# Score matmuls of half the height for the first 8 pairs and of full height for the rest, x^T of two batches by DMA, and a table of urgencies, in a kernel of attention and a gated MLP

## The chip, the cores and the metric

One core of a Trainium2 chip. The metric is the device time of one execution in microseconds (us); a comparison uses the median of several runs. Of the engines, TensorE (PE) does the matmuls, VectorE (DVE), ScalarE (ACT) and GpSimd (POOL) the work on their results, and SyncE (SP) issues transfers. PE's clock is granted at one of two levels, 1.2 or 2.4 GHz; the profile gives it as a share of 2.4 GHz.

## The reference

q, k and v have the shape [4, 8, 768, 64]: 4 batches of 8 heads. Each query keeps the 6 chunks of 32 keys with the greatest upper bound on the score, computed from each chunk's smallest and greatest key. The result feeds a gated MLP.

```python
k_min = np.min(k_chunks, axis=3); k_max = np.max(k_chunks, axis=3)
ub = np.sum(np.maximum(q[:, :, :, None, :] * k_min[:, :, None, :, :],
                       q[:, :, :, None, :] * k_max[:, :, None, :, :]), axis=-1)
ub = np.where(causal, ub, -1e9)
top_chunks = np.argsort(ub, axis=-1)[..., -6:]
scores = scale * np.matmul(q, k.transpose(0, 1, 3, 2))     # kept where selected and causal
x = softmax(scores) @ v                                    # then [4, 768, 512]
h = gelu(x @ w_in)                                         # w_in [512, 1024]
u, v = h[..., :512], h[..., 512:]
v_n = (v - mean(v)) / sqrt(var(v) + 1e-6) * g_ln
v_s = einsum('ts,bsd->btd', w_sg, v_n) + b_sg              # w_sg [768, 768]
out = x + (u * v_s) @ w_out                                # w_out [512, 512]
```

## The kernel before

The work is written as operations (`P.op`), each with an engine, an estimated cost, the data that it reads and writes, and a priority. `Program.schedule` plays them through with these costs: whenever an engine is free, it starts the operation that can start first, and among those within 0.02 us of it the one with the smallest priority. That gives one fixed order for each engine; `link` adds the semaphore waits that the data need. So the order on the chip is decided ahead, and where the costs are off, an engine waits in that order. Each engine takes its instructions in order, the transfers that SP or POOL issue included.

The heads are taken in pairs (16 pairs, one head in partitions 0 to 63, the other in 64 to 127) and in quads of two pairs. The steps of a pair:

- `loads`: k, q and v of two heads, six transfers of SP. There are 3 buffers of each kind, and at most 4 loads are in flight.
- `kside`, `qside`: PE transposes in f32; DVE takes minimum and maximum of the chunks (W), ACT copies to KT (bf16) and qT (f32), DVE makes rT, POOL casts qT to QT. `vside`: POOL casts v to vx.
- `select`, for a quad: bounds on PE with tiles of 64 x 32, then on DVE transposition, the 6th greatest value of each query (`max`), a comparison and a transposition to Dt: 24 rows for each head, 1 where a chunk is not selected.
- `scores`: for six pieces (`PIECES`) of the causal triangle, K^T Q over 64 rows, and on top of it a matmul of the indicator IND (-BIG for the keys of a chunk) with Dt, also over 64 rows. The two heads of a pair use the two halves of PE's rows. Queries below LO = 192 need no mask. ACT takes the exp of each piece into E; POOL zeroes what lies over the diagonal.
- `head`: 21 matmuls of E with v, then DVE divides into XS. `xtrans`: x^T of a pair, 6 PE transposes and a DVE copy to xT.

After the four pairs of a batch come `moe_h` (hv and hu with w_in, gelu on ACT, statistics and vhat on DVE, one step on POOL for rstd) and `moe_g` (the matmul with w_sg, two DVE steps to uT, the matmul with w_out, the sum with XS, the output). The buffers of MoE are double, by the batch's parity. The priorities are 100 for each quad, plus fixed offsets:

```python
                if g % 2 == 0:
                    b = g // 2 - 1
                    P.base = 100.0 * (g - 1) + 150.0 + 40
                    moe_h(b)
                    P.base = 100.0 * (g - 1) + 150.0 + 150
                    moe_g(b)
```

`weights(h)` issues the transfers of w_in, w_sg and w_out on POOL's queue, two for a head, once the first exp of the pair is done ("tick"); the bias and g_ln go by SP. Until the first scores PE runs matmuls on zeros in its free time (`fill`).

Of the kernel before, what the change touches and what calls it, by code (L numbers as in the profile page):

```python
# [43 lines left out]
class Op:  # L44
    __slots__ = ("eng", "fn", "cost", "prio", "deps", "dma", "ps", "alloc", "table", "burst",
                 "start", "end", "pos", "waits", "inc", "count", "idx", "lane", "bulk", "port")


class Program:
# [54 lines left out]
    def schedule(self):  # L104
# [23 lines left out]
        table = None  # L128
        burst_left = {}
# [18 lines left out]
        soft_free = 0.0  # L148
        flight = []
        held = {"pool": 0.0, "dve": 0.0}  # L150
        while n < len(ops):
            pick = None
            for e in ENGINES:
# [22 lines left out]
                best = min((c for c in cands if c[0] <= tmin + 0.02), key=lambda c: c[1])  # L176
# [16 lines left out]
            cost = o.cost  # L193
            if e == "act" and o.table is not None:
# [180 lines left out]
def pe(cols, n=1):  # L375
    return max(cols / 2400.0, n * 0.027)


def _kernel(nc, q, k, v, w_in, g_ln, w_sg, b_sg, w_out, out):
# [24 lines left out]
    for c_, ps_ in enumerate(PIECES):  # L404
# [5 lines left out]
        ELEN.append(o_)  # L410

    with contextlib.ExitStack() as ctx:
# [12 lines left out]
        XS = T("XS", [128, 2 * NT, DM], BF16)  # L425
# [7 lines left out]
        DIRECT = 4  # L433
        qn = [T(f"qn{i}", [128, NT, 2, DH], F32) for i in range(NQS)]
# [3 lines left out]
        rT = [T(f"rT{i}", [128, NSEL], F32) for i in range(4)]  # L438
# [3 lines left out]
        KT = [T(f"KT{i}", [128, S], BF16) for i in range(4)]  # L442
        QT = [T(f"QT{i}", [128, S], BF16) for i in range(4)]
# [3 lines left out]
        Dt = [T(f"Dt{i}", [128, NSEL], BF16) for i in range(2)]  # L447
        E = [[T(f"E{i}_{c}", [128, 2, n], BF16) for c, n in enumerate(ELEN)] for i in range(2)]
# [47 lines left out]
        def weights(h):  # L496
            after = [("tick", h)]
            for i in (2 * h, 2 * h + 1):
                if i < 4:
                    P.op("pool", lambda g, i=i: g.dma_start(  # L500
                        winb[:, i, :], bass.AP(w_in.tensor, 128 * DFF * i, [[DFF, 128], [1, DFF]])), 2.0,
                        reads=after, writes=[("winb", i)], dma=f"winb{i}")
                elif i < 10:
                    j = i - 4
                    P.op("pool", lambda g, j=j: g.dma_start(
                        wsgf[j], bass.AP(w_sg.tensor, 128 * S * j, [[S, 128], [1, S]])), 1.6,
                        reads=after, writes=[("wsgf", j)], dma=f"wsgf{j}")
# [376 lines left out]
```

## Time and profile before

| | |
|---|---|
| median of 3 runs | 266.33 us (264.33 to 268.38) |
| the profiled execution | 266.45 us |
| its span, first to last instruction | 264.7 us |
| busy: PE / DVE / ACT / POOL | 232.8 / 188.9 / 148.7 / 70.8 us |
| moved by DMA | 28.72 MB, 109 GB/s over the span |

Busy time is the time in which an engine has work in it; matmuls overlap, so a busy PE may still have room. A chain of waits followed back from the last instruction tells which work ended last at each step.

### The profile page before, as it was taken

The page shows a single profiled execution, that of the slowest core. Times are in us where ns is not written, and L with a number is a line of the kernel's source. Part 1 is how long each engine was busy: PE and PEld are TensorE (multiplying, and loading weights), DVE is VectorE, ACT ScalarE, POOL GpSimd, SP SyncE. Part 2 cuts the span into 40 slices and gives each one's busy share as a digit, 9 for nine tenths or more (in the row PEclk, how much of TensorE's full clock was granted, in tenths as well). Part 3 has the DMA queues.
Part 4 walks back from the last instruction along what each step waited for, and adds up shares of the span by engine and source line. Part 5 has one row for each costly group of instructions (what it writes and reads, how often), then busy time and mean ns, then how long its engine had stood idle before and what let it go on. Part 6 is the DMA issues. An engine that isn't in the chain of part 4 may idle for free.

```text
span 264.7 us, 6262 instructions
## 1 busy us (share of the span) xinstructions
PE 232.8 (88%) x2534; PEld 132.1 (50%) x2551; DVE 188.9 (71%) x541; ACT 148.7 (56%) x224; POOL 70.8 (27%) x95
## 2 busy tenths in 40 slices
PE   8998788698999999988977999978988998689884
PEld 3554455546546665455534765544435565434431
DVE  3659666478769978867597768866687776447783
ACT  1316799268549658477655857197674554736000
POOL 4135551936120423225021313143011021001000
PEclk9999999599999999999999999999999999979999
DMA  7999999998983166865022050210000032100033
GB/s 165 208 226 207 219 221 200 194 235 185 220 177 88 34 198 147 215 156 122 5 59 59 2 178 2 82 41 4 2 0 0 5 119 81 40 0 0 2 119 120
DMA packets 81437, 28.72 MB, mean 109 GB/s; under 512 B 76416, under 2 KB 77696, under 8 KB 81408
## 3 DMA queue, kind: packets, MB, share of 16 engines
q1 hardware_dynamic: 79392, 25.57, 40.6%
q0 software_dynamic: 2016, 2.75, 6.2%
q8 instruction: 20, 0.33, 0.5%
q14 instruction: 9, 0.07, 0.1%
HBM read 24.77 MB, written 6.29 MB: 117 GB/s over the span
## 4 chain that ended last, share of the span: by engine, by line
PE 51%; DMA 16%; DVE 14%; issue 8%; ACT 7%; SPq 1%; POOL 1%; POOLq 1%; DVEq 0%
DMA kn<-in_k_dram 11%; PE PSG L767 8%; PE PSG L787 8%; PE PSG L674 6%; PE PSC L633 6%; DMA vn<-in_v_dram 5%; PE PSG L723 5%; PE PSG L595 5%; DVE vhat L739 5%; PE PSC L639 4%; PE PSG L542 3%; DVE vsT L774 3%; DVE uT L778 2%; ACT E_1 L649 2%; PE PSG L695 2%
## 5 line engine op out<-in xcount | busy, mean ns | idle before, releaser
L633 PE MATMUL PSC<-QT,KT 64*128 64x128 bf16 (+3 forms) x384 | 40.3, 265 | 8.3 <-ACT E_1 L649 2.4
L548 DVE TENSOR_REDUCE W<-PSG 128x12 f32<-128x384 f32 x64 | 32.7, 541 | 8.3 <-PE PSG L542 8.2
L767 PE MATMUL PSG<-wsgT,vhat 128*128 128x384 bf16 x192 | 35.3, 327 | 3.4 <-DVE vhat L739 3.3
L639 PE MATMUL PSC<-Dt,IND 64*128 64x128 bf16 (+5 forms) x352 | 37.8, 260 | 0.0
L633 PEld LDWEIGHTS PSC<-QT,KT 64*128 64x128 bf16 x384 | 17.1, 95 | 28.5 <-issue 7.3
L657 POOL TENSOR_SCALAR_AFFINE_SELECT E_0<-E_0 128x1024 bf16<-128x1024 bf16 x16 | 17.9, 1121 | 39.0 <-ACT E_0 L649 39.0
L576 POOL CAST QT<-qT 128x768 bf16<-128x768 f32 x16 | 14.2, 895 | 49.2 <-PE PSC L639 25.3
L649 ACT ACTIVATE E_1<-PSC 128x1024 bf16<-128x1024 f32 x16 | 16.4, 1024 | 17.7 <-PE PSC L639 17.7
L649 ACT ACTIVATE E_0<-PSC 128x1024 bf16<-128x1024 f32 x16 | 16.6, 1035 | 17.1 <-PE PSC L639 17.1
L774 DVE SCALAR_TENSOR_TENSOR vsT<-PSG,glnT,bsgbc 128x384 f32<-128x384 f32 x32 | 19.6, 612 | 9.0 <-PE PSG L767 8.9
L767 PEld LDWEIGHTS PSG<-wsgT,vhat 128*128 128x128 bf16 x192 | 17.2, 98 | 17.6 <-ACT uT L754 2.7
L787 PE MATMUL PSG<-woutb,uT 128*128 128x512 bf16 x88 | 22.2, 380 | 3.7 <-DVE uT L778 3.0
L749 PE MATMUL PSG<-xT,winb 128*128 128x384 bf16 x128 | 24.1, 327 | 0.1
L723 PE MATMUL PSG<-winb,xT 128*128 128x512 bf16 x89 | 22.2, 391 | 1.6 <-DVE xT L699 1.1
L793 DVE TENSOR_TENSOR osb<-PSG,XS 128x512 f32<-128x512 f32 x24 | 16.4, 689 | 8.9 <-PE PSG L787 8.7
L727 ACT ACTIVATE vgb<-PSG 128x512 f32<-128x512 f32 x24 | 14.0, 596 | 15.4 <-PE PSG L723 15.4
L551 ACT ACTIVATE KT<-PSG 128x384 bf16<-128x384 f32 x32 | 15.3, 497 | 11.7 <-DVE W L548 11.6
L649 ACT ACTIVATE E_3<-PSC 128x1024 bf16<-128x1024 f32 x16 | 16.5, 1031 | 6.9 <-PE PSC L639 6.9
L570 ACT ACTIVATE qT<-PSG 128x384 f32<-128x384 f32 x32 | 15.1, 504 | 9.3 <-PE PSG L565 9.3
L580 POOL CAST vx<-vn 128x768 bf16<-128x768 f32 x16 | 13.6, 848 | 24.6 <-PE PSG L674 14.1
L754 ACT ACTIVATE uT<-PSG 128x384 bf16<-128x384 f32 x32 | 15.7, 490 | 7.9 <-PE PSG L749 7.4
L649 ACT ACTIVATE E_4<-PSC 128x1024 bf16<-128x1024 f32 x16 | 16.6, 1037 | 6.2 <-PE PSC L639 6.1
(77 smaller groups left out, 449.1 us busy)
## 6 DMA issues: line engine op xcount, KB each, us to landing
kn<-in_k_dram SPq DMA_DIRECT2D x32, 192.0 KB, 3.6
qn<-in_q_dram SPq DMA_DIRECT2D x32, 192.0 KB, 3.7
vn<-in_v_dram SPq DMA_DIRECT2D x32, 192.0 KB, 3.6
out_dram<-osb SPq DMA_DIRECT2D x24, 256.0 KB, 2.0
winb<-in_moe_w_in_dram POOLq DMA_DIRECT2D x4, 256.0 KB, 5.5
vhat<-in_moe_w_sg_dram POOLq DMA_DIRECT2D x3, 192.0 KB, 4.6
uT<-in_moe_w_sg_dram POOLq DMA_DIRECT2D x3, 192.0 KB, 5.7
woutb<-in_moe_w_out_dram POOLq DMA_DIRECT2D x4, 128.0 KB, 6.3
```

Of the source, the lines that this page charges most:

```text
L548: P.op("dve", lambda d, t=t, m=m, op=op, hf=hf: d.tensor_reduce(W[w][:, m, 12 * hf:12 * hf + 12], t.ap()[:, 0:TG].rearrange("p (c x) -> p ...
L633: r = e.matmul(t.ap()[:, 512 * i + o:512 * i + o + n], KT[w][rows, 128 * kb:128 * kb + 128], QT[w][rows, q0:q0 + n], start=first, stop=(q0 ...
L639: r = e.matmul(t.ap()[:, 512 * i + o + m0 - q0:512 * i + o + n], ind[rows, 128 * kb:128 * kb + 128], Dt[u][rows, m0 - LO:q0 + n - LO], sta ...
L649: P.op("act", lambda e, t=t, c=c, n=n: e.activation(E[es][c][:], t.ap()[:, 0:1024].rearrange("p (i x) -> p i x", x=512)[:, :, 0:n], ACTF.E ...
L657: P.op("pool", lambda g, ev=ev, m=m: g.affine_select(ev, ev, pattern=[[0, 2], [0, m], [1, 128]], compare_op=ALU.is_ge, fill=0.0, base=0, c ...
L674: r = e.matmul(t.ap()[:, 65 * qb:65 * qb + 65], E[es][c][:, i, o:o + 128], vx[w][:, kb, i, :], start=first, stop=(c == 0), skip_group_chec ...
L723: r = e.matmul(t.ap()[:, 0:F], xT[s][:, dk, 128 * qt:128 * qt + 128], winb[:, dk, F:DFF], start=(dk == 0), stop=(dk == NDK - 1))
L749: r = e.matmul(t.ap()[:, 0:TG], winb[:, dk, 128 * fb:128 * fb + 128], xT[s][:, dk, TG * tg:TG * tg + TG], start=(dk == 0), stop=(dk == NDK ...
L767: r = e.matmul(t.ap()[:, 0:TG], vhat[s][:, sb, 128 * fb:128 * fb + 128], wsgT[:, sb, TG * tg:TG * tg + TG], start=(sb == 0), stop=(sb == N ...
L774: P.op("dve", lambda d, t=t, fb=fb, tg=tg, vs=vs: d.scalar_tensor_tensor(vsT[vs][:], t.ap()[:, 0:TG], glnT[:, fb:fb + 1], bsgbc[:, TG * tg ...
L787: r = e.matmul(t.ap()[:, 0:DM], gT[s][:, fb, 128 * qt:128 * qt + 128], woutb[:, fb, :], start=(fb == 0), stop=(fb == NF - 1))
L793: P.op("dve", lambda d, t=t, qt=qt, os_=os_: d.tensor_tensor(osb[os_][:], t.ap()[:, 0:DM], XS[:, (b % 2) * NT + qt, :], op=ALU.add), dve(D ...
```

## The change

- `scores` stays for the pairs 0 to 7 (SIDE = 8). From pair 8 on `scores_one` works on one head at a time: the first head's operands KA and QA hold K^T or Q^T in rows 0 to 63 and the indicator or Dt in rows 64 to 87, the second head's KB and QB hold them in rows 64 to 127 and in rows 0 to 23 (the rest is zero), so one matmul gives score and mask. The rows that come from other partitions are copied by SP: KB, the indicator, QB, and two of Dt, five transfers for a pair. A head has three tiles (1024, 1024 and 640 columns), the diagonal blocks first, and E is one buffer.
- x^T of the batches 2 and 3 is made by `dma_start_transpose` on SP, but for the last slice of batch 3. XS has the blocks of 128 features outside.
- A table URGENCY gives each step of each pair or batch its own priority, in place of the fixed offsets.
- The weights: each pair releases a list (WHEN), and the bias and g_ln are released by pair 2.
- The plan's constants: latencies, costs of operations and transfers, a cost for a change between kinds of matmul (MODE_SWITCH), and a tolerance for each engine (SLACK) within which the priority decides. rT has two buffers in place of four.

```diff
-LAT = {"pe": 0.15, "act": 0.20, "dve": 0.12, "pool": 0.15, "sp": 0.05}
+LAT = {"pe": 0.15, "act": 0.25, "dve": 0.12, "pool": 0.15, "sp": 0.05}
+SLACK = {"pe": 0.15, "act": 0.1, "dve": 0.1, "pool": 0.3, "sp": 0.02}
 TABLE_SWITCH = 1.3
+MODE_SWITCH = 0.095
...
-                best = min((c for c in cands if c[0] <= tmin + 0.02), key=lambda c: c[1])
+                best = min((c for c in cands if c[0] <= tmin + SLACK[e]), key=lambda c: c[1])
...
+            if e == "pe" and o.mode != mode:
+                cost += MODE_SWITCH
+                mode = o.mode
...
-                if e == "pool":
-                    soft_free = max(soft_free, t + 1.0) + 2.0 * cost
-                    dma_free = max(dma_free, t + 0.3) + 0.4 * cost
-                else:
-                    dma_free = max(dma_free, t + 0.3) + cost
-                free[e] = max(t + 0.6, dma_free - 3.0) if e == "sp" else t + 0.9
-                o.end = (soft_free if e == "pool" else dma_free) + 2.0
+                dma_free = max(dma_free, t + (1.0 if e == "pool" else 0.2)) + cost
+                free[e] = t + (0.9 if e == "pool" else 0.5)
+                o.end = dma_free + (2.2 if e == "pool" else 1.6)
...
+WHEN = [(0, 1), (2, 3, 4, 5), (6, 7, 8, 9, 14), (10, 11, 12, 13)]
+URGENCY = {
+        "load": [21, 1, 120, 126, 221, 388, 525, 392, 525, 361, 529, 668, 611, 889, 862, 904],
+        "k": [320, 143, 76, 123, 147, 316, 75, 314, 315, 432, 551, 578, 604, 684, 879, 859],
+        "q": [30, 132, 97, -60, 230, 303, 441, 411, 1100, 493, 579, 1201, 1307, 1169, 1501, 1463],
+        "loadv": [-95, 74, 163, 188, 369, 485, 389, 414, 630, 365, 923, 913, 1121, 705, 597, 897],
+        "v": [-64, -18, 111, -54, 217, -39, 255, 47, 223, 239, 571, 414, 620, 954, 1074, 1042],
+        "sel": [59, 94, 184, 412, 259, 490, 252, 594],
+        "sc": [133, 165, 273, 364, 398, 448, 500, 430, 429, 771, 686, 924, 1027, 1076, 919, 955],
+        "pv": [189, 319, 361, 325, 520, 489, 535, 637, 840, 1086, 1098, 1136, 1309, 1349, 1344, 1305],
+        "xt": [-417, -44, -42, 194, -297, 173, 130, -226, 110, 773, 703, 802, 893, 1227, 1006, 1369],
+        "wsg": [-130],
+        "hv": [43, 609, 856, 831],
+        "hu": [404, -196, 1218, 1970],
+        "pt": [617, 508, 743, 1334, 1292, 1441, 2245, 1650],
+        "out": [423, 540, 506, 541, 584, 822, 1099, 421],
+}
...
+    ECUT = [(0, 1024), (1024, 2048), (2048, 2688)]
+    ETOT = 2688
+    FOFF = []
+    acc = S
+    for kb_ in range(NT - 1):
+        FOFF.append(acc)
+        acc += S - 128 * (kb_ + 1)
...
+        for u in range(2):
+            P.op("dve", lambda d, u=u: d.memset(Dt[u][:, 0:LO], 0.0), 0.1, writes=[("Dt0", u)])
+        for i in range(4 if SIDE < 16 else 0):
+            P.op("pool", lambda g, i=i: g.memset(QB[i][0:64, :], 0.0), 0.5, prio=400.0, writes=[QB[i].name + "D"])
+            P.op("pool", lambda g, i=i: g.tensor_copy(KB[i][0:64, :], IND[0][0:64, :]), 0.8, prio=400.0,
+                 reads=["IND0"], writes=[KB[i].name + "I"])
...
-        def weights(h):
-            after = [("tick", h)]
-            for i in (2 * h, 2 * h + 1):
+        def weights(p):
+            after = [("tick", p)]
+            for i in WHEN[p]:
...
-            if h == 1:
-                P.op("sp", lambda s: s.dma_start(bsgbc[:], bass.AP(b_sg.tensor, 0, [[0, 128], [1, S]])),
-                     1.5, writes=["bsgbc"], dma="bsg")
-                P.op("sp", gln_load, 0.3, writes=["glnT"], dma="gln")
+                else:
+                    P.op("sp", lambda s: s.dma_start(bsgbc[:], bass.AP(b_sg.tensor, 0, [[0, 128], [1, S]])),
+                         2.3, reads=after, writes=["bsgbc"], dma="bsg")
+                    P.op("sp", gln_load, 0.3, reads=after, writes=["glnT"], dma="gln")
...
+            if p < SIDE:
+                return
+            P.op("sp", lambda e: e.dma_start(KB[w][64:128, :], KA[w][64:128, :]), 0.4,
+                 reads=[("KAI", w)], writes=[("KB", w)], dma=f"kb{w}")
+            P.op("sp", lambda e: e.dma_start(KA[w][64:64 + NC, :], IND[0][0:NC, :]), 0.2,
+                 reads=["IND0", ("KB", w)], writes=[("KAI", w)], dma=f"ki{w}")
...
+            if p >= SIDE:
+                P.op("sp", lambda e: e.dma_start(QB[w][64:128, :], QA[w][64:128, :]), 0.4,
+                     reads=[("QAD", w)], writes=[("QB", w)], dma=f"qb{w}")
...
+            for j in range(4):
+                p = 2 * g + j % 2
+                w = p % 4
+                if p < SIDE:
+                    continue
+                qt_, lo, key = (QA[w], 64, ("QAD", w)) if j < 2 else (QB[w], 0, QB[w].name + "D")
+                P.op("sp", lambda e, j=j, qt_=qt_, lo=lo: e.dma_start(qt_[lo:lo + NC, :],
+                                                                      Dt[u][32 * j:32 * j + NC, :]), 0.2,
+                     reads=[("Dt", u), ("Dt0", u)] + ([("QB", w)] if j < 2 else []), writes=[key],
+                     dma=f"D{w}_{j // 2}")
...
+        def scores_one(p, i):
+            w, es = p % 4, p % 2
+            kt_, qt_, rows = (KA[w], QA[w], slice(0, 64 + NC)) if i == 0 else (KB[w], QB[w], slice(0, 128))
+            rd = [("KA", w, 0), ("KA", w, 1), ("KAI", w), ("QA", w), ("QAD", w)] if i == 0 else \
+                [("KB", w), KB[w].name + "I", ("QB", w), QB[w].name + "D"]
+            pieces = [(128 * kb, 128, kb, 128 * kb) for kb in range(NT)]
+            pieces += [(FOFF[kb], S - 128 * (kb + 1), kb, 128 * (kb + 1)) for kb in range(NT - 1)]
+            for c, (c0, c1) in enumerate(ECUT):
+                t = ps_score.tile()
+                mms = []
+                for (e0, n, kb, q0) in pieces:
+                    a, z = max(e0, c0), min(e0 + n, c1)
+                    while a < z:
+                        y = min(z, c0 + ((a - c0) // 512 + 1) * 512)
+                        mms.append((a - c0, y - a, kb, q0 + a - e0))
+                        a = y
+
+                def sc(e, t=t, mms=mms):
+                    for (o, n, kb, q0) in mms:
+                        r = e.matmul(t.ap()[:, o:o + n], kt_[rows, 128 * kb:128 * kb + 128],
+                                     qt_[rows, q0:q0 + n], start=True, stop=True, skip_group_check=True)
+                    return r
+                P.op("pe", sc, sum(max(m_[1], 66) for m_ in mms) / 2400.0 + 0.03, reads=rd, writes=[t], alloc=t)
+                P.op("act", lambda e, t=t, c0=c0, c1=c1: e.activation(
+                    E[es][:, ETOT * i + c0:ETOT * i + c1], t.ap()[:, 0:c1 - c0], ACTF.Exp, scale=SCALE),
+                    act(c1 - c0), reads=[t], writes=[("E", es, 3 * i + c)], ps=[t], table="exp")
+            ev = E[es][:, ETOT * i:ETOT * i + S].rearrange("p (j x) -> p j x", x=128)
+            P.op("pool", lambda g: g.affine_select(ev, ev, pattern=[[0, NT], [1, 128]], compare_op=ALU.is_ge,
+                                                   fill=0.0, base=0, channel_multiplier=-1), gps(S),
+                 reads=[("E", es, 3 * i)], writes=[("E", es, 3 * i)])
 
...
+            r, w = [("XS", b % 2, 2 * dk), ("XS", b % 2, 2 * dk + 1)], [("xT", b % 2, dk)]
+            if b >= XDMA and not (dk == NDK - 1 and b == B - 1):
+                P.op("sp", lambda e: e.dma_start_transpose(
+                    xT[b % 2][:, dk, :].rearrange("p (j x) -> p j x", x=128),
+                    XS[:, b % 2, dk].rearrange("p j x -> p (j x)")), 1.0, reads=r, writes=w, dma=f"x{dk}")
+                return
...
+                for p in (2 * g - 2, 2 * g - 1):
+                    at("sc", p)
+                    if p < SIDE:
+                        scores(p)
+                    for i in range(2):
+                        if p >= SIDE:
+                            at("sc", p)
+                            P.base += 10 * i
+                            scores_one(p, i)
+                        at("pv", p)
+                        P.base += 10 * i
+                        head(2 * p + i)
+                    if p < len(WHEN):
+                        P.base = 0.0
+                        weights(p)
+                    if p == 3:
+                        at("wsg", 0)
                         for sb in range(NT):
                             wsg_trans(sb)
-                    if h % 2 == 1:
-                        P.base += 5
-                        xtrans(h // H, (h % H) // 2)
+                    at("xt", p)
+                    xtrans(p // 4, p % 4)
```

## Rows read from the trace of the kernel before

**Rows 1.** The page: busy time by engine, and PE's granted clock in 40 slices.

```profile
PE 232.8 (88%) x2534; PEld 132.1 (50%) x2551; DVE 188.9 (71%) x541; ACT 148.7 (56%) x224; POOL 70.8 (27%) x95
...
PEclk9999999599999999999999999999999999979999
```

**Rows 2.** Stretch, length; busy PE, PEld, DVE, ACT, POOL; PEclk, DMA share, GB/s.

```profile
22.00:66.00 44.00, 36.52 (x535) 23.24 (x537) 30.63 (x100) 31.50 (x49) 25.15 (x35) 0.92 1.06 210
47.00:57.00 10.00, 8.49 (x112) 5.40 (x114) 5.37 (x12) 3.73 (x5) 8.17 (x13) 0.66 1.11 207
66.00:228.00 162.00, 148.40 (x1709) 85.44 (x1720) 122.64 (x348) 101.41 (x150) 37.72 (x42) 1.00 0.33 84
228.00:264.70 36.70, 27.73 (x178) 12.98 (x178) 22.88 (x46) 9.82 (x17) 1.32 (x1) 0.95 0.11 44
```

**Rows 3.** The chain that ended last: start us, us, what.

```profile
37.71 7.39 DMA vn<-in_v_dram
45.12 3.30 DMA kn<-in_k_dram
...
242.49 2.84 DVE vhat L739 x6
```

**Rows 4.** Waits, 22 to 66 us: who for whom, us, times, longest.

```profile
POOL vx L580 <- DMA vn<-in_v_dram: 7.5, 1, 7.5
...
PE PSG L542 <- DMA kn<-in_k_dram: 3.0, 1, 3.0
```

**Rows 5.** Waits from 228 us to the end.

```profile
PE PSG L787 <- DVE uT L778: 2.4, 2, 1.6
...
PE PSG L723 <- DVE xT L699: 1.1, 1, 1.1
```

**Rows 6.** Timeline of PE, 223 to 226 us: start, length, what, count.

```profile
224.18 0.27 PE L633 MATMUL PSC<-QT,KT 64*128 64x256 bf16 x2
224.29 0.27 PE L639 MATMUL PSC<-Dt,IND 64*128 64x256 bf16 x2
224.50 0.30 PE L674 MATMUL PSG<-vx,E_2 128*128 128x65 bf16 x4
...
225.03 0.29 PE L674 MATMUL PSG<-vx,E_0 128*128 128x65 bf16 x4
225.25 0.39 PE L633 MATMUL PSC<-QT,KT 64*128 64x512 bf16 x2
```

**Rows 7.** Timeline of PE: first and last of 28 runs of scores.

```profile
113.73 0.23 PE L633 MATMUL PSC<-QT,KT 64*128 64x128 bf16 x2
...
226.98 0.34 PE L633 MATMUL PSC<-QT,KT 64*128 64x384 bf16 x2 [0.27 <-ACT E_2 L649]
```

**Rows 8.** Timeline, transposes of batch 2's last slice to hv.

```profile
183.18 0.51 PE L695 MATMUL PSG<-identB,XS 128*128 128x128 bf16 x6
...
183.62 0.69 PE L595 MATMUL PSG<-qT,W 64*32 64x288 f32 x8
...
184.95 0.81 PE L723 MATMUL PSG<-winb,xT 128*128 128x512 bf16 x3 [0.16 <-issue]
```

**Rows 9.** Groups by line: the copy to xT; busy us, mean ns | idle.

```profile
L699 DVE COPY xT<-PSG 128x768 bf16<-128x768 bf16 x16 | 8.9, 555 | 6.2 <-PE PSG L695 5.9
```

**Rows 10.** Outputs (L796): time from issue to landing.

```profile
DMA to landing us min/median/max: 2.0/2.0/3.1
```

**Rows 11.** Loads of q, k and v (L527): time to landing.

```profile
DMA to landing us min/median/max: 2.5/3.6/10.3
```

**Rows 12.** Timeline: Dt of pairs 8 and 9, pair 8's first score.

```profile
115.88 0.78 DVE L618 STREAM_TRANSPOSE Dt<-Dn 128x576 bf16<-128x576 bf16 x1
...
118.21 0.28 PE L633 MATMUL PSC<-QT,KT 64*128 64x128 bf16 x4 [0.63 <-ACT E_4 L649]
```

**Rows 13.** Waits of SP's queue.

```profile
SPq L527 <- POOL vx L580: 13.1, 2, 10.9
```

More of the change, by code (lines that the diff above doesn't have):

```diff
@@ L45 @@
     __slots__ = ("eng", "fn", "cost", "prio", "deps", "dma", "ps", "alloc", "table", "burst",
-                 "start", "end", "pos", "waits", "inc", "count", "idx", "lane", "bulk", "port")
+                 "start", "end", "pos", "waits", "inc", "count", "idx", "lane", "bulk", "port", "mode")
 class Program:
@@ L128, in schedule @@
         table = None
+        mode = "full"
         burst_left = {}
@@ L437, in _kernel @@
         qT = [T(f"qT{i}", [128, S], F32) for i in range(4)]
-        rT = [T(f"rT{i}", [128, NSEL], F32) for i in range(4)]
+        rT = [T(f"rT{i}", [128, NSEL], F32) for i in range(2)]
         W = [T(f"W{i}", [128, 2, 32], F32) for i in range(4)]
@@ L441, in _kernel @@
         vx = [T(f"vx{i}", [128, NT, 2, DH + 1], BF16) for i in range(4)]
-        KT = [T(f"KT{i}", [128, S], BF16) for i in range(4)]
-        QT = [T(f"QT{i}", [128, S], BF16) for i in range(4)]
+        KA = [T(f"KA{i}", [128, S], BF16) for i in range(4)]
+        KB = [T(f"KB{i}", [128, S], BF16) for i in range(4)]
+        QA = [T(f"QA{i}", [128, S], BF16) for i in range(4)]
+        QB = [T(f"QB{i}", [128, S], BF16) for i in range(4)]
         U = [T(f"U{i}", [128, NBLK, 32], F32) for i in range(2)]
@@ L645, in scores @@
                 n = ELEN[c]
[L646 to L647 removed]
+                P.op("pe", sc, 2 * n / 2400.0 + 0.02, mode="rows",
+                     reads=[("KA", w, 0), ("KA", w, 1), ("QA", w), ("Dt", u), "IND0", "IND0b", "IND1"],
                      writes=[t], alloc=t)
[L649 to L650 removed]
+                ev = E[es][:, off:off + 2 * n].rearrange("p (i x) -> p i x", i=2)
@@ L651, in scores @@
+                off += 2 * n
+                P.op("act", lambda e, t=t, n=n, ev=ev: e.activation(
+                    ev, t.ap()[:, 0:1024].rearrange("p (i x) -> p i x", x=512)[:, :, 0:n], ACTF.Exp,
                     scale=SCALE), act(2 * n), reads=[t],
-                    writes=[("E", es, c)] + ([("tick", 2 * p), ("tick", 2 * p + 1)] if c == 0 else []), ps=[t],
-                    table="exp")
+                    writes=[("E", es, c)] + ([("tick", p)] if c == 0 else []), ps=[t], table="exp")
@@ L665, in head, with block @@
             t = ps_g.tile((3,) if h < H else (2, 3))
-            def pv(e):
-                first = True
-                for c in (2, 3, 4, 5, 1, 0):
-                    for kb, q0, n in PIECES[c]:
-                        for x in range(0, n, 128):
-                            qb = (q0 + x) // 128
-                            o = EOFF[kb, qb][1]
-                            r = e.matmul(t.ap()[:, 65 * qb:65 * qb + 65], E[es][c][:, i, o:o + 128],
-                                         vx[w][:, kb, i, :], start=first, stop=(c == 0), skip_group_check=True)
-                            first = False
-                return r
-            P.op("pe", pv, 21 * 0.03, reads=[("E", es, c) for c in range(6)] + [("vx", w), ("vx1", w)],
+            def block(kb, qb):
+                if p >= SIDE:
+                    return ETOT * i + (128 * qb if kb == qb else FOFF[kb] + 128 * (qb - kb - 1))
+                c, o = EOFF[kb, qb]
+                return 2 * sum(ELEN[:c]) + ELEN[c] * i + o
+            order = [(kb, qb) for kb in range(NT) for qb in range(kb + 1, NT)] + [(kb, kb) for kb in range(NT)]
+            def pv(e):
+                for n, (kb, qb) in enumerate(order):
+                    o = block(kb, qb)
+                    r = e.matmul(t.ap()[:, 65 * qb:65 * qb + 65], E[es][:, o:o + 128], vx[w][:, kb, i, :],
+                                 start=(n == 0), stop=(kb == qb), skip_group_check=True)
+                return r
+            keys = range(6) if p < SIDE else range(3 * i, 3 * i + 3)
+            P.op("pe", pv, 0.63, reads=[("E", es, c) for c in keys] + [("vx", w), ("vx1", w)],
                  writes=[t], alloc=t)
@@ L761, in moe_g @@
             for tg in range(2):
+                at("pt", 2 * b + tg)
                 for fb in range(NF):
@@ L781, in moe_g @@
                         writes=[("uT", s, fb, tg)])
+                at("out", 2 * b + tg)
                 for qt in range(3 * tg, 3 * tg + 3):
@@ L814, in _kernel @@
                 select(g)
             if g >= 1:
-                for j in range(4):
-                    h = 4 * (g - 1) + j
-                    P.base = 100.0 * (g - 1) + 150.0 + 10 * j
-                    if j % 2 == 0:
-                        scores(h // 2)
-                    head(h)
-                    if h < 8:
-                        weights(h)
-                    if h == 5:
+                for p in (2 * g - 2, 2 * g - 1):
[3 more added lines that the diff above has]
+                    for i in range(2):
+                        if p >= SIDE:
+                            at("sc", p)
[9 more added lines that the diff above has]
+                        at("wsg", 0)
```

88 lines of the change are left out of this document (48 added, 40 removed).

## Prediction

> **What bounds the kernel now.** I read the busy shares first. TensorE (PE) is busy 88% of the span, no other engine over 71%, and its clock dips twice, at about a fifth of the span and near its end [rows 1]. The mean hides three stretches, so next I cut the span at 22, 66 and 228 us [rows 2]. From 22 to 66 us the DMA engines are saturated (share 1.06, 210 GB/s) while PE is busy 36.52 of 44 us: 7.5 us idle. Its granted clock falls to a mean of 0.66 in 47 to 57 us, so 0.68 of those 10 us were at the lower of its two levels (1.2 of 2.4 GHz), half of which, 3.4 us, is lost. Front loss: 10.9 us. From 66 to 228 us PE is busy 148.40 of 162 us: PE is the bound there and 13.6 us are idle. From 228 us to the end PE is busy 27.73 of 36.70 us: 9.0 us idle, and a mean clock of 0.95 costs 0.05 x 2 x 36.7 / 2 = 1.8 us. Tail loss: 10.8 us. Then I asked the chain who ends last: at the front it runs through loads of v and k, and in the tail through the six vhat operations of VectorE (DVE) [rows 3]. The waits agree: in front PE waits 3.0 us for a k load and GpSimd (POOL) 7.5 us for a v load [rows 4]; in the tail PE waits for uT and xT, both made by DVE [rows 5]. So three things are worth something: PE time in the middle, the order of transfers in front, and work that could lie beside the waits of the last batch.
>
> **The change, part by part.** The sum is made against the profiled execution, 266.45 us (span 264.7); the median of the three runs, 266.33, is 0.1 lower.
>
> **Full-height scores, pairs 8 to 15.** A half-height pair of matmuls, one for each head, runs together: two of 256 columns start at 224.18 and the next two at 224.29, 256 columns for both heads in 0.11 us, one a cycle at 2.4 GHz [rows 6]. A pair has 2688 score and 2432 mask columns (counted from PIECES, less the queries under LO), 5120 / 2.4 GHz = 2.13 us. Full height, the mask's 24 rows ride in the same pass as the 64 of the head, so each head takes 2688 columns alone: 5376, 2.24 us. That is 0.11 us more for a pair, 0.85 us for eight. What it removes is the change between the two kinds of matmul. Two 256-column matmuls that start at 224.29 have been fed by 224.40, yet the next PV matmul starts at 224.50; the four that start at 225.03 follow each other every 0.031 us (21 from 224.50 to 225.15), and the score behind them starts at 225.25 [rows 6]. So 0.10 us goes at each entry and each exit. From 113.73 us on the scores stand in 28 separate runs, the first of them pair 7's alone, so 27 for the pairs 8 to 15; only the last run begins with a wait for ScalarE (ACT) [rows 7]. 27 x 2 x 0.09 = 4.9 us, less 0.85, is 4.0 us of PE time. Not all of it is on the path: PE is busy 92% in the middle, and 13 tiles inside these runs wait for an exp anyway, so that a gap less there buys nothing. I take -3.0; bounds: -4.6 (0.10 for all 54) to +0.9 (all gaps covered, only the columns left). Exp and mask keep their size: six exps and some 1.7 us of POOL for a pair, as before. A head's PV can now start when its own three exps are done, which I count under order.
>
> **x^T by DMA, seven of the last eight.** Each removes six PE transposes, 0.44 us from 183.18 to the next work at 183.62 [rows 8], and a DVE copy of 555 ns [rows 9]: 7 x 0.44 = 3.1 us of PE and 3.9 us of DVE. Added is a transfer of 192 KB from SBUF to SBUF on SyncE (SP), a kind that the trace doesn't show. Nearest rows: 256 KB from SBUF land in 2.0 us at median, 3.1 at most [rows 10]; loads take 3.6 at median and 10.3 at most [rows 11]. The second half moves little (DMA share 0.33 over the middle [rows 2]), so I lean to [rows 10] and take 3 to 4 us. Five of the seven lie far ahead of their use. The last of batch 2 doesn't: there PE starts the transposes at 183.18 and hv at 184.95, 1.8 us later [rows 8], so hv(2) moves back by some 2 us, and by 8.5 at the worst row; PE has the pairs of batch 3 in between. In batch 3 the last slice stays on PE. I take -2.0; bounds -3.9 to +8.5. The Trainium skill ("DMA: Bandwidth & Descriptors", section "Latency and other measured facts") gives transposing transfers some 261 GB/s; 192 KB would then move in 0.75 us, an estimate from that page, and with it this term would be -3. No run here shows it yet, and the sum does without it.
>
> **Forty small copies on SP** (K and Q of the second head, the indicator, two of Dt, for eight pairs). They are new steps between Dt and the scores. In the trace pair 8 has the least room: Dt is ready at 116.66 and its first score tile starts at 118.21, 1.55 us later and after a wait for an exp [rows 12]; a copy of 2.0 to 3.1 us [rows 10] is late by 0.4 to 1.5 us there. The other three quads had room of over 4 us. SP takes its queue in order, and behind a copy that waits for Dt stand loads and outputs. I take +1.0, between 0 and +6 (1.5 for each of four quads). POOL gets four memsets and four copies more, some 5 us by the plan's costs, at a time of its choosing; it is idle most of the span, and where that cover is missing they delay a cast by about 1 us. Two rT buffers instead of four cost nothing as long as quads are over 10 us apart, as their Dt are.
>
> **Weights and loads in front.** Before, the first exp of pair 0 releases all four chunks of w_in (2 MB read: 10 us at 210 GB/s [rows 2]); now two, with the others, w_sg and w_out moved one pair back, and the bias with its 0.4 MB no longer stands among the first loads but waits in SP's queue for pair 2. This is what the k and v loads of [rows 4] queued behind. The first loads gain nothing: v of pair 0 now goes ahead of q and k and is as large as the bias was. Of the front loss of 10.9 us I take half, -5; bounds -10.9 to +4 (v too early holds k back by one pair of loads more).
>
> **Order in the tail.** The old plan gave MoE of a batch a fixed place 40 and 150 behind its pairs; by 223 us batch 2 is done and batch 3 has nothing beside it. In the table the sgu matmuls of batches 1 and 2 (1334, 1292, 1441) stand behind the scores of the last pairs (919 to 1076), so there is work left to lie beside the wait for xT, rstd, vhat and uT [rows 5]. The chain itself stays: xT, hv, gelu, statistics, vhat, sgu, out. Of 10.8 us I take -4; bounds -9 to +3.
>
> **Order in the middle.** 13.6 us idle, which a table may use better or worse: -2, bounds -8 to +6. A table whose plan has wrong transfer times does the latter.
>
> **Sum:** 266.45 - 3.0 - 2.0 + 1.0 - 5.0 - 4.0 - 2.0 = 251.45, or **251.3 us** as a median, 5.6% faster. Two thirds of it are order, which can't be read off one edit.
>
> **The rivals.**
> *Order works in full* (0.20): the middle's PE terms come whole (-4.0 - 3.1), copies +1, front -9, tail -7, middle -4: 240 us. For: the losses are all waits with work elsewhere to put beside them. Against: the tail's chain and the first 22 us have little to move.
> *PE time turns into waits* (0.20): what leaves PE is waited for elsewhere, exps in the long runs, DVE in the tail; front and tail keep their form: -1.0 - 1.0 + 1.0 - 1.0 = 264 us. For: DVE is busy 122.64 of 162 us in the middle [rows 2], and 13 tiles wait for exp. This is also the case in which the plan's order doesn't come true on the chip.
> *SP holds the loads back* (0.12): a copy or transposing DMA that waits for Dt, QA or XS stands ahead of k and v loads. SP has waited 10.9 us once for a cast [rows 13], and what late loads cost shows in 47 to 57 us: 1.5 us idle and 3.4 us of clock [rows 2], with the idle before it (3.0 us in [rows 4]) some 6 us each time. It decides once more than two of the four late quads starve like that; four times is +24 against -10 that remain: about 280 us.
>
> **How the numbers follow.** My forecast, 246 to 258, has 0.48. A measurement of this kernel tells about 2% from no change (261.0 to 271.7). Faster by more: 0.48 + 0.20 + a quarter of the second rival = 0.73; within: 0.15; slower: 0.12. The range from 239 to 267 leaves out the SP rival (0.12) and the better part of the first (0.08).
>
> **What would show it.** Scores of late pairs as matmuls over 88 or 128 rows, following PV matmuls without the 0.10 us gap; six PE transposes left in batches 2 and 3; transposing DMAs that land in 2 to 4 us; PE idle from 22 to 66 us under 4 us with a clock near 1.0; idle in the last 37 us under 6 us; first score of each late quad within 3 us of Dt or unhurried. The forecast is wrong if hv(2) waits for a transposing DMA, if SP's waits for Dt or XS run to over 5 us with PE starving behind them, or if the front's DMA-bound stretch ends as late as before.

## The result, and the profile after

| | before | after |
|---|---|---|
| median of 4 runs | 265.33 us (264.20 to 268.38) | 253.02 us (250.04 to 256.35) |
| the profiled execution, its span | 266.45, 264.7 us | 250.04, 248.3 us |

The ratio is 0.9476, 95% interval 0.934 to 0.961: 5.2% faster, where 5.6% was forecast. The ratios here leave disturbed runs out, so they are not the quotients of the medians. The profiled execution is 16.4 us shorter, and PE is busy 13.7 us less in it; 3.2 of these are only fewer matmuls on zeros at the start (14.6 to 11.4 us).

The page of after, busy time and PE's clock as in [rows 1]:

```profile
PE 219.1 (88%) x2340; PEld 131.7 (53%) x2354; DVE 192.3 (77%) x536; ACT 147.5 (59%) x224; POOL 77.5 (31%) x103
...
PEclk9999889999999999999999999999999999999999
```

PE's share is the same 88%. The dip at a fifth of the span has become a shallow one, and that near the end is gone in this execution. The stretches of after, columns as in [rows 2], the last one shorter by the gain:

```profile
22.00:66.00 44.00, 39.23 (x604) 24.32 (x606) 32.23 (x100) 34.47 (x50) 25.64 (x34) 0.96 1.09 216
66.00:228.00 162.00, 149.56 (x1564) 92.38 (x1575) 131.83 (x363) 106.69 (x163) 38.48 (x43) 1.00 0.45 106
228.00:248.30 20.30, 13.03 (x69) 5.91 (x67) 13.02 (x22) 0.00 (x0) 0.00 (x0) 0.98 0.20 78
```

In front PE idles 4.8 us instead of 7.5, with the DMA engines as full as before. Fixed times don't show a stage that moves, so I marked each batch by its first hv matmul in the PE timelines:

| first hv of batch | 0 | 1 | 2 | 3 | end of span |
|---|---|---|---|---|---|
| before | 65.9 | 126.1 | 184.9 | 233.3 | 264.7 |
| after | 63.4 | 124.0 | 175.2 | 215.8 | 248.3 |

The front gave 2.5 us and the way from batch 0's hv to batch 3's 15.0 us (167.4 to 152.4). Behind batch 3's hv nothing came: 31.4 us before, 32.5 after. What now stands ahead of that hv, in the PE timeline of after:

```profile
204.08 1.14 PE L869 MATMUL PSG<-wsgT,vhat 128*128 128x384 bf16 x6
205.06 0.88 PE L741 MATMUL PSC<-QA,KA 88*128 88x384 bf16 x7
205.77 0.81 PE L768 MATMUL PSG<-vx,E 128*128 128x65 bf16 x21
206.42 1.14 PE L869 MATMUL PSG<-wsgT,vhat 128*128 128x384 bf16 x6
...
212.89 1.67 PE L890 MATMUL PSG<-woutb,uT 128*128 128x512 bf16 x7 [0.95 <-DVE uT L880]
...
215.82 5.35 PE L823 MATMUL PSG<-winb,xT 128*128 128x512 bf16 x24
```

Batch 2's sgu (L869) and out matmuls (L890) lie between the last pairs' scores (L741) and PV (L768); only one of these rows begins with a wait. The scores are 88 rows high, and seven of them (1664 columns, 0.69 us at 2.4 GHz) are followed after 0.71 us: no gap as in [rows 6] is left. By the same timelines, each matmul's time to the next start less the idle in between, scores fell from 45.7 to 43.1 us, transposes for x^T from 7.0 to 3.4, and idle time from 27.5 to 19.1. (After's side of these three is from the changed kernel's second profile, e_after below: span 248.2 us.)

The new transfers on SP; first those of x^T, with issue time on SP and landing time:

```profile
L786 SPq DMA_TRANSPOSE xT<-XS x7: 1219/1242/2316, 123.4 to 207.4; - x7
...
DMA to landing us min/median/max: 2.7/2.8/4.5
```

And the timeline of one quad's Dt to its first score:

```profile
139.18 0.76 DVE L666 STREAM_TRANSPOSE Dt<-Dn 128x576 bf16<-128x576 bf16 x1
...
140.72 1.61 SPq L674 DMA_DIRECT2D QA<-Dt  x2
...
143.34 1.05 PE L741 MATMUL PSC<-QA,KA 88*128 88x128 bf16 x11 [2.96 <-DMA QA<-Dt]
```

x^T lands in 2.8 us at the median, a little under the 3 to 4 us of the forecast, and in 4.5 at most; each transfer holds SP for 1.2 us of issuing at the median, 2.3 at most. Ahead of them SP stands still for 19.0 us in all, most of it in these two groups of its waits:

```profile
SPq L786 <- DVE vsT L876: 10.5, 3, 5.1
SPq L786 <- DVE XS L778: 5.7, 3, 5.0
```

Dt is ready at 139.94; two copies to QA take SP from 140.72 to 142.33, and PE waits 2.96 us. It is the only wait for such a copy, and not all of it is the copy's. At the same place h_half16, a run below without these copies, waits for an exp; its row, then ACT's rows in after:

```profile
145.13 0.28 PE L692 MATMUL PSC<-QA,KA 64*128 64x128 bf16 x4 [2.37 <-ACT E L710]
```

```profile
139.71 1.28 ACT L745 ACT_TABLE_LOAD   x1
141.01 1.62 ACT L745 ACTIVATE E<-PSC 128x1024 bf16<-128x1024 f32 x2
```

In both runs ACT first loads its table of functions, for 1.28 us, and the first exp behind it ends at 142.03 in after (141.01 and 1.02 for the first of the two). If the scores need that exp there too, as they do in h_half16, some 1.65 us of the 2.96 would have been waited for anyway and 1.3 fall to the copies: an estimate from these rows.

### The profile page after: what moved, and what is told of

The parts are those of the page before. It is cut to its first block, busy times and chain, and to the rows that moved or that the text cites. A ratio compares the mean times of both kernels' runs of the same rounds, so it can differ in the third digit from the quotient of the medians.

```text
span 248.3 us, 5930 instructions
## 1 busy us (share of the span) xinstructions
PE 219.1 (88%) x2340; PEld 131.7 (53%) x2354; DVE 192.3 (77%) x536; ACT 147.5 (59%) x224; POOL 77.5 (31%) x103
## 4 chain that ended last, share of the span: by engine, by line
PE 46%; DVE 27%; DMA 12%; issue 7%; ACT 4%; POOL 1%; SPq 1%; POOLq 1%; DVEq 0%
PE PSG L869 8%; PE PSG L890 7%; PE PSG L643 6%; PE PSG L768 5%; DMA qn<-in_q_dram 5%; PE PSC L741 4%; DVE vhat L839 4%; PE PSC L692 3%; DVE uT L880 3%; DMA kn<-in_k_dram 3%; DMA vn<-in_v_dram 3%; DVE stats L830 3%; DVE vsT L876 3%; PE PSG L823 3%; DVE W L586 2%
## 5 line engine op out<-in xcount | busy, mean ns | idle before, releaser
L745 ACT ACTIVATE E<-PSC 128x1024 bf16<-128x1024 f32 (+1 forms) x48 | 42.0, 923 | 25.3 <-PE PSC L741 25.2
L710 ACT ACTIVATE E<-PSC 128x1024 bf16<-128x1024 f32 (+1 forms) x48 | 42.1, 926 | 16.7 <-PE PSC L698 16.7
L869 PE MATMUL PSG<-wsgT,vhat 128*128 128x384 bf16 x192 | 35.4, 326 | 3.8 <-DVE XS L778 2.7
L768 PE MATMUL PSG<-vx,E 128*128 128x65 bf16 x672 | 25.6, 194 | 0.8 <-DVE XS L778 0.7
L890 PE MATMUL PSG<-woutb,uT 128*128 128x512 bf16 x89 | 21.8, 379 | 5.0 <-DVE uT L880 4.0
L749 POOL TENSOR_SCALAR_AFFINE_SELECT E<-E 128x768 bf16<-128x768 bf16 x16 | 13.8, 863 | 39.2 <-ACT E L745 39.2
L869 PEld LDWEIGHTS PSG<-wsgT,vhat 128*128 128x128 bf16 x192 | 17.3, 97 | 16.2 <-DVE XS L778 3.4
L768 PEld LDWEIGHTS PSG<-vx,E 128*128 128x128 bf16 x672 | 23.4, 98 | 4.0 <-DVE XS L778 0.9
L620 POOL CAST QA<-qT 128x768 bf16<-128x768 f32 x16 | 13.7, 857 | 32.9 <-ACT qT L614 29.3
L823 PE MATMUL PSG<-winb,xT 128*128 128x512 bf16 x91 | 21.6, 379 | 0.9 <-issue 0.6
L589 ACT ACTIVATE KA<-PSG 128x384 bf16<-128x384 f32 x32 | 15.6, 495 | 11.2 <-DVE W L586 11.2
L692 PE MATMUL PSC<-QA,KA 64*128 64x128 bf16 (+2 forms) x192 | 19.7, 263 | 1.8 <-ACT E L710 1.6
L827 ACT ACTIVATE vgb<-PSG 128x512 f32<-128x512 f32 x24 | 14.3, 598 | 10.8 <-PE PSG L823 10.7
L830 DVE BATCH_NORM_STATS2 stats<-vgb 128x6 f32<-128x512 f32 x24 | 16.3, 683 | 5.4 <-ACT vgb L827 5.0
L880 DVE TENSOR_TENSOR uT<-vsT,uT 128x384 bf16<-128x384 f32 x32 | 19.7, 617 | 0.8
L628 POOL CAST vx<-vn 128x768 bf16<-128x768 f32 x16 | 13.8, 864 | 20.9 <-PE PSG L768 16.4
L614 ACT ACTIVATE qT<-PSG 128x384 f32<-128x384 f32 x32 | 15.6, 502 | 7.0 <-PE PSG L609 7.0
```

The source lines that it names most:

```text
L692: r = e.matmul(t.ap()[:, 512 * i + o:512 * i + o + n], KA[w][rows, 128 * kb:128 * kb + 128], QA[w][rows, q0:q0 + n], start=first, stop=(q0 ...
L710: P.op("act", lambda e, t=t, n=n, ev=ev: e.activation(ev, t.ap()[:, 0:1024].rearrange("p (i x) -> p i x", x=512)[:, :, 0:n], ACTF.Exp, sca ...
L745: P.op("act", lambda e, t=t, c0=c0, c1=c1: e.activation(E[es][:, ETOT * i + c0:ETOT * i + c1], t.ap()[:, 0:c1 - c0], ACTF.Exp, scale=SCALE ...
L768: r = e.matmul(t.ap()[:, 65 * qb:65 * qb + 65], E[es][:, o:o + 128], vx[w][:, kb, i, :], start=(n == 0), stop=(kb == qb), skip_group_check ...
L823: r = e.matmul(t.ap()[:, 0:F], xT[s][:, dk, 128 * qt:128 * qt + 128], winb[:, dk, F:DFF], start=(dk == 0), stop=(dk == NDK - 1))
L830: P.op("dve", lambda d, qt=qt, st=st: d.bn_stats(stats[st][:], vg[qt]), dve(F), reads=[("vg", qt)], writes=[("stats", st)])
```

## The experiments

My theory: the gain is mostly order, and the scores without gaps and x^T by DMA are worth some 2 us each. The rivals: the edits only turn PE time into waits; the copies and transposing transfers on SP cost what the edits bring. SIDE is the first pair with full-height scores (16: none), XDMA the first batch whose x^T goes by DMA (4: none). Ratios are to the kernel before on the same chip. Only a_half and b_ends keep after's order on every engine; in the others the plan is made anew.

| | edit to after | ratio [95%] | median us |
|---|---|---|---|
| a_half | late scores over 64 rows, no mask | 0.9542 [0.9474, 0.9610] | 259.27 |
| b_ends | end waits for outputs alone | 0.9345 [0.9302, 0.9388] | 250.74 |
| c_offsets | old offsets for the table | 0.9623 [0.9569, 0.9678] | 257.39 |
| d_table | SIDE 16, XDMA 4 | 0.9417 [0.9371, 0.9464] | 252.38 |
| e_after | none | 0.9443 [0.9376, 0.9509] | 252.28 |
| f_release | SIDE 16, XDMA 4, old offsets | 0.9763 [0.9692, 0.9834] | 260.62 |
| g_xpe | XDMA 4 | 0.9392 [0.9336, 0.9449] | 250.45 |
| h_half16 | SIDE 16 | 0.9524 [0.9462, 0.9585] | 254.39 |
| i_best | XDMA 4, end waits for outputs | 0.9324 [0.9256, 0.9393] | 250.22 |
| j_consts | f_release, old WHEN, bias first | 0.9825 [0.9766, 0.9885] | 262.63 |
| k_x15 | XDMA 0 | 1.0016 [0.9961, 1.0072] | 268.69 |
| l_pool | i_best, Dt copied by POOL | 0.9498 [0.9444, 0.9552] | 253.69 |

The medians before were 268.25 us (a to d), 267.61 (e to h) and 266.93 (i to l). Times below that are worked out from ratios take 267 us for before.

The runs a to d were made on one chip and e to l on another, and the kernel before did not run alike on the two. In the runs that the ratios use it took 268.3 us at the mean on the first, with granted clocks of 0.973 to 0.981, and 266.6 on the second (e to h), with 0.973 to 0.994. The ratios of a to d may be up to 0.6% too low for that, so where a step crosses the chips I also give it by plain means of the same runs: 256.1 (a), 250.6 (b), 258.2 (c), 252.7 (d), 251.8 (e), 260.1 (f), 250.4 (g), 253.9 (h).

### What the gap costs: a_half

```diff
-  e.matmul(..., kt_[rows, ...], qt_[rows, ...])
+  e.matmul(..., kt_[64*i:64*i+64, ...], qt_[64*i:64*i+64, ...])
```

> The changed kernel with every instruction in the same order, but the scores of pairs 8 to 15 run over 64 rows in place of 88 or 128; the masking of unselected chunks in these pairs is left out. Columns and plan are the same, only the change between kinds of matmul comes back, 32 times in and out. If a change costs 0.09 us that the path feels: 32 x 2 x 0.09 = 5.8 us of PE time, and 3 to 5 us of the total, 256 to 258 us. If the gaps were covered by waits anyway: within 1 us of the changed kernel's 253.

The PE timeline of a_half, the same four steps as in after above:

```profile
207.72 1.15 PE L869 MATMUL PSG<-wsgT,vhat 128*128 128x384 bf16 x6
208.80 0.88 PE L741 MATMUL PSC<-QA,KA 64*128 64x384 bf16 x7
209.61 0.82 PE L768 MATMUL PSG<-vx,E 128*128 128x65 bf16 x21
210.27 1.14 PE L869 MATMUL PSG<-wsgT,vhat 128*128 128x384 bf16 x6
```

From sgu to scores 1.08 us instead of 0.98, from scores to PV 0.81 instead of 0.71; PV takes the same 0.65 (0.66). So 0.10 us goes at each entry and exit, as read from [rows 6], with the same columns in the same order. The Trainium skill ("TensorEngine Tiling (Array Packing)", Key Properties) says that a change of the tiling mode drains the engine; these rows agree and give the size. In time: 1.0% over e_after by the ratios (2.6 us), 4.3 us by plain means, 4.4 us between the profiled executions (span 252.6 to e_after's 248.2, mean clock 0.982 and 0.985). The intervals overlap (0.9474 to 0.9509), and a_half's runs spread widely, 254.30 to 263.37 us, so the size is rough. 32 runs of scores have 64 entries and exits, 6.4 us at 0.10: part of it is waited for anyway.

### Table against edits: c_offsets, d_table, f_release, e_after

```diff
-  P.base = URGENCY[kind][i]
+  (the offsets of the kernel before)          # c_offsets, f_release
-  SIDE = 8; XDMA = 2
+  SIDE = 16; XDMA = 4                         # d_table, f_release
```

> The changed kernel with the fixed offsets of the kernel before in place of the table of urgencies; scores, x^T, release of the weights and plan constants as changed. By the prediction the order is worth two thirds of the gain, of which the release of the weights stays here: 253 + 6 to 9 = 259 to 262 us. Rival, by the busy times (PE 13.7 us less busy, 2.7 us less idle): the edits themselves give the gain, 253 to 256 us.

> The changed kernel with all 16 pairs at half height and all x^T by PE: table, release and constants alone. By the prediction the three edits are worth 4 us: 257 us. Rival (the edits are the gain): 262 us or more. If the copies eat what the scores save: 253 to 255.

> Fixed offsets, all scores at half height, all x^T by PE: of the change only the release of the weights and the plan's constants. By the prediction that is the front term, -5 us: 0.98 of the kernel before. If the 0.962 of the run with offsets came from scores and x^T, this is 1.00; if it came from release and constants, 0.96.

> The changed kernel itself, beside the next three on one chip: 0.948 of the kernel before.

| | old offsets | table | table's worth |
|---|---|---|---|
| neither edit | 0.9763 (f) | 0.9417 (d) | -9.2 us |
| both edits | 0.9623 (c) | 0.9443 (e) | -4.8 us |
| edits' worth | -3.7 us | +0.7 us, intervals overlap | |

By the ratios the two edits bring the 4 us forecast for them (-3.0 - 2.0 + 1.0) under the old offsets, and nothing that shows under the table; taking the two intervals together (half-widths 0.0067 and 0.0046, root of the squares 0.008) the step from d to e lies between -1.5 and +2.9 us. But c and d ran on the one chip, e and f on the other. By plain means the edits are worth -1.9 us under the old offsets and -0.9 under the table, and the table -7.4 and -6.5. So the table's worth of 5 to 9 us holds either way (on one chip, f to h, the table with x^T by DMA brings -6.4, intervals apart); that the edits are worth less under it is not shown. What the table does alone is seen where batch 3 begins, first in the PE timeline of f_release:

```profile
221.03 0.34 PE L692 MATMUL PSC<-QA,KA 64*128 64x384 bf16 x2 [0.27 <-ACT E L710]
...
223.14 1.45 PE L768 MATMUL PSG<-vx,E 128*128 128x65 bf16 x42 [0.91 <-ACT E L710]
...
225.52 0.51 PE L794 MATMUL PSG<-identB,XS 128*128 128x128 bf16 x6 [0.93 <-DVE XS L778]
226.69 5.36 PE L823 MATMUL PSG<-winb,xT 128*128 128x512 bf16 x24 [0.65 <-DVE xT L798]
```

The old offsets leave a chain of waits: exp, XS, xT, hv. In d_table there is work in them:

```profile
215.96 1.15 PE L869 MATMUL PSG<-wsgT,vhat 128*128 128x384 bf16 x6
216.94 1.70 PE L768 MATMUL PSG<-vx,E 128*128 128x65 bf16 x42
218.93 1.90 PE L890 MATMUL PSG<-woutb,uT 128*128 128x512 bf16 x8 [0.30 <-DVE XS L778]
220.67 0.50 PE L794 MATMUL PSG<-identB,XS 128*128 128x128 bf16 x6
221.01 1.03 PE L890 MATMUL PSG<-woutb,uT 128*128 128x512 bf16 x4
222.09 5.35 PE L823 MATMUL PSG<-winb,xT 128*128 128x512 bf16 x24
```

Batch 2's sgu and out stand between PV, transposes and hv, and hv comes 4.6 us earlier, which is the whole difference of these two executions (span 257.5 and 252.9). This is order alone: the scores here are half-height and x^T is made by PE.

### The rest of the plan: j_consts

```diff
-WHEN = [(0, 1), (2, 3, 4, 5), (6, 7, 8, 9, 14), (10, 11, 12, 13)]
+WHEN = [(0, 1, 2, 3), (4, 5, 6, 7), (8, 9, 10, 11), (12, 13)]   # and bias, g_ln at the start
```

> Fixed offsets, half height, x^T by PE, and the weights and the bias released as in the kernel before: only the plan's constants are those of the change. By the prediction the release of the weights is the front's gain, so this is 1.00 of the kernel before. Rival, by the first MoE matmul, which the run with release and constants starts at 66.1 us as the kernel before did at 65.9: the release gives nothing and the constants give all, 0.97 to 0.98.

The planner's new costs, with the new buffers, bring 1.75% alone (4.7 us); the later release of the weights 0.6% more (1.7 us), with overlapping intervals. In the profiled executions the first hv stands at 69.6 us in j_consts, 66.1 in f_release and 63.9 in d_table: the release helps in front, and the table as well. In the total the release's share is not resolved.

### Each edit under the table: g_xpe, h_half16, k_x15

```diff
-  SIDE = 8
+  SIDE = 16     # h_half16
-  XDMA = 2
+  XDMA = 4      # g_xpe;   XDMA = 0: k_x15
```

> The changed kernel with all x^T by PE. By the prediction 2 us slower than the changed one (0.955 of the kernel before). Rival: the PE time that the transfers save is not missed, and SP without seven transposing transfers of 1.2 us is no worse: 0.945 to 0.95.

> The changed kernel with all scores at half height. By the prediction 2 us slower than the changed one (-3 for the scores, +1 for the copies): 0.955. Rival: the copies cost what the scores save (one wait for a copy of Dt is 3.0 us in the changed trace): 0.94 to 0.95.

> The changed kernel with 15 of the 16 slices of x^T by DMA in place of 7. By the prediction each saves PE time: 2 us faster than the changed kernel, 0.935. If each transposing transfer costs some 0.2 us on SP, as the runs without them say: 1.5 to 3 us slower, 0.95 to 0.955.

Full height with its copies: h to e -2.2 us (intervals overlap by 0.005), d to g -0.7 (by plain means -2.3); neither is resolved alone. x^T by DMA: d to h +2.9 us (by plain means +1.2) and, on one chip, g to e +1.4; with the intervals taken together +0.8 to +4.9 and -1.0 to +3.7. The forecast of -2.0 is outside both. That x^T by DMA costs time is not shown beyond doubt; that it does not bring 2 us is. k_x15 makes 15 slices by DMA instead of 7 and loses 15 us. Its line of the transposing transfers, its SP timeline, its stretch from 22 to 66 us and one of its PE waits (at 128.98 us), one after the other:

```profile
L786 SPq DMA_TRANSPOSE xT<-XS x15: 1211/1312/4909, 42.4 to 223.1; - x15
...
DMA to landing us min/median/max: 2.7/3.8/10.0
```

```profile
42.37 3.89 SPq L786 DMA_TRANSPOSE xT<-XS  x1
...
50.68 4.91 SPq L786 DMA_TRANSPOSE xT<-XS  x1
```

```profile
22.00:66.00 44.00, 35.24 (x516) 22.46 (x515) 28.48 (x89) 28.70 (x42) 24.48 (x33) 0.84 1.13 201
```

```profile
PE PSG L850 <- DMA xT<-XS: 3.6, 1, 3.6
```

Where the DMA engines are full (share 1.13), one such transfer holds SP for up to 4.9 us, with loads of k and v behind it, and the slowest lands after 10.0. PE is 4.0 us less busy there than in after, its clock is 0.84 instead of 0.96, and the first hv comes at 73.9 us instead of 63.4. This fits the third rival's mechanism, though the plan too is made anew here. In after the first x^T transfer goes out at 123.4 us, in the stretch with a DMA share of 0.45.

### The end: b_ends and i_best

```diff
-  for d, idxs in self.dma_sems.items():
-      eng.wait_ge(dsem[d], 16 * len(idxs))
+  for d in [d for d in self.dma_sems if d[0] == "o"]:
+      eng.wait_ge(dsem[d], 16 * len(self.dma_sems[d]))
```

> The changed kernel, whose SP queue waits at the end for the three output counters alone and not for all 61 transfer counters. Theory: the span ends 4.2 us after the last sum in the changed kernel and 2.5 us in the one before because SP runs through 24 more waits; then this is 1.7 us or more faster, about 251. Rival: the last output itself lands later, and nothing changes, 253.

> The changed kernel with all x^T by PE and with the last waits of SP cut to the three output counters; each was 0.5 to 1% faster by itself. If the two add: 0.93 of the kernel before. If both were chance: 0.945.

The last outputs in after (span 248.3), then in b_ends (span 248.4), timelines of SP and DVE:

```profile
242.34 2.15 SPq L900 DMA_DIRECT2D out_dram<-osb  x3
...
243.45 0.69 DVE L896 TENSOR_TENSOR osb<-PSG,XS 128x512 f32<-128x512 f32 x1 [0.27 <-PE PSG L890]
```

```profile
244.05 2.16 SPq L900 DMA_DIRECT2D out_dram<-osb  x3
...
245.15 0.69 DVE L896 TENSOR_TENSOR osb<-PSG,XS 128x512 f32<-128x512 f32 x1 [0.27 <-PE PSG L890]
```

After's last sum is done at 244.14 and the span ends 4.2 us later; in b_ends 2.6 us later. SP's program ends with one wait for each DMA counter. From the last matmul to the end it takes 3.2 us with 37 counters (before, d_table, f_release; 3.6 in j_consts), 3.5 with 41 (h_half16), 4.4 with 57 (g_xpe), 4.9 with 61 (after, e_after; 4.7 in c_offsets, 4.5 in k_x15), and 3.3 and 3.2 with three (b_ends, i_best). So twenty-four more waits cost 1.3 to 1.7 us, 0.05 to 0.07 each; as 37 take no longer than three, they seem to be hidden behind the last output's landing. b_ends is 1% below e_after in ratio (2.6 us; the intervals overlap by 0.001), but the two ran on two chips, and it is 1.1 us by plain means; the profiled executions are equally long (span 248.4 and 248.2). What is shown is the shorter end. i_best, without the transposing transfers too, has the lowest ratio of all, 6.8% below before; its upper end, 0.9393, lies 0.002 inside e_after's interval.

### Copies of Dt by POOL: l_pool

```diff
-  P.op("sp", lambda e: e.dma_start(qt_[lo:lo+NC, :], Dt[u][...]), 0.2, ..., dma=...)
+  P.op("pool", lambda e: e.tensor_copy(qt_[lo:lo+NC, :], Dt[u][...]), gps(S), ..., lane=1)
```

> As the first run of this call, and the 32 copies of Dt to QA and QB made by POOL in place of transfers on SP. If the copies by DMA cost 2 to 3 us (a wait of 2.7 us for one stands in the changed trace, and each holds SP for 0.8 us): 0.92 to 0.925. If POOL's casts and masks, which now stand behind 0.85 us for each copy, are late in turn: 0.93 or above.

It is 4.6 us slower than i_best (0.9498 to 0.9324, intervals apart), so the copies' time is not to be had back on POOL: my theory that they cost 2 to 3 us by DMA found no support. The groups of POOL in l_pool by line:

```profile
L674 POOL COPY QB<-Dt 24x768 bf16<-24x768 bf16 x8 | 7.4, 928 | 0.5
L674 POOL COPY QA<-Dt 24x768 bf16<-24x768 bf16 x8 | 6.6, 829 | 16.3 <-DVE Dt L666 8.8 <-DVE rstd L834 7.2
```

A copy takes 0.83 to 0.93 us, and POOL stood idle for Dt 8.8 us in all. What lies behind such a copy in POOL's order, casts and the zeroing of E, waits with it. I infer that the wait moved from SP to POOL; no run separates it from the new plan.

## Why the prediction came out right, point by point

| term | forecast | measured |
|---|---|---|
| order in all (front, middle, tail) | -11 | -15.6: constants -4.7, release -1.7, table -9.2 (267 us x the steps from 1 to j, f, d); with the table by plain means (-7.4), -13.8 |
| full-height scores with copies | -3.0 + 1.0 | -2.2 (h to e) |
| x^T by DMA | -2.0 | +2.9 (d to h; by plain means +1.2) |
| sum | -15.0 | -14.9 = 267 x (1 - 0.9443) |

The time fell into the forecast's 246 to 258 us by luck, through two errors that cancel: order brought some 3 to 5 us more than forecast, x^T by DMA as much less.

*Full height* was right in mechanism: 0.10 us at each change of height and no gap left. A pair's scores take 0.19 us less on PE (2.73 for the pairs 0 to 7, 2.54 for 8 to 15 in after's timeline); that holds only the gaps behind scores, and those in front lie in the time of what precedes them (PV 22.9 us in d_table, 21.7 in g_xpe). The size, -2.2 us net against -2.0, agrees but is not resolved by either pair of runs. *The copies* cost one wait for Dt, of whose 2.96 us some 1.3 are theirs by the estimate above, near the 1.5 that I had given to a late quad, and something not in the sum at all: their 20 counters make SP's last waits 1.2 us longer (g_xpe against d_table).

*x^T by DMA* is the term that failed: "I take -2.0". PE was rid of 3.6 us of transposes, and the transfers landed about as forecast, yet none of the 2 us came. Five of the seven were said to lie far ahead of their use; what I didn't price is that SP issues them in order, 1.2 us each, and waits with other transfers behind it: 19.0 us in all in after, up to 5.1 at once, and in h_half16 36.3 us, up to 13.0. What these waits cost PE no run separates. Four more counters at the end are 0.3 us of it (h_half16 against d_table); how the rest splits between SP's queue, the changed plan and the two chips stays open. The estimate from the transfer rate that the forecast gave aside, 0.75 us, is not borne out either: the shortest took 2.7 us to land, and with that shorter time the term would have been further off.

*Order* was undersized and misplaced. "Of 10.8 us I take -4" for the tail: behind batch 3's hv nothing was gained (31.4 and 32.5 us, of which 1.7 are SP's added last waits; 30.8 in d_table without them). The chain from xT over vhat and uT to out is the same, and the two uT waits are still there, 2.4 us as in [rows 5]. The gain lies ahead of that hv, where batch 2's MoE now fills the last pairs' waits. The front's -5 came as -2.5 in the profiled execution (-4.1 in e_after's), and the release alone, on which it was argued, is not resolved in the total. Which rows of the table do it no run separates.

*The rivals.* That PE time turns into waits may be what happened to the two edits under the table (+0.7 us by the ratios, -0.9 by plain means), though not to the order. SP holding back the loads to PE's cost was not seen in after, but k_x15 is a case of it, 15 us slower. The order in full, 240 us, asked for a shorter tail.

## What to carry to other kernels

In a kernel whose order is planned ahead, the plan can be worth more than the edits: 13.8 to 15.6 us here, against at most 3.7 for two edits that each took work off the busiest engine. The worth of an edit may belong to the order in which it is made; a square of four runs tells, but only with all four on one chip, which mine were not. A wait put down to a new step may have been there without it: look at the same place in a run that lacks the step. A transfer that relieves a busy engine is paid in the issuing queue's time, in what stands behind it, and in one more wait at the end of the program.

## What the hardware showed that I had not expected

- SP takes about 0.05 to 0.07 us for each counter that it waits for at the end; 24 more of them cost 1.3 to 1.7 us.
- A transposing transfer of 192 KB takes 1.2 us of SP to issue at the median in after (2.3 at most, DMA share 0.45), and up to 4.9 us in k_x15 with the DMA engines full (share 1.13), with up to 10.0 to land.
- A copy of 24 partitions to another place in SBUF, 36 KB, holds SP for 0.8 us (1.61 for two in the timeline above), longer than the 0.55 us of the 64-partition copy just ahead of it (QB from QA, 96 KB, 140.07 us).
